# Moving TensorE's weight operands inside their SBUF buffers, in a chain of attention and two expert layers

## The chip, the core and the metric

The program runs on one NeuronCore of a Trainium2 chip. The metric is device time in microseconds (us) of one execution, from the first to the last instruction with what lies around them. Three timed executions of the kernel before stand beside one profiled execution, and the profile tells where the time of that one went.

## The reference

```python
def _attn_ref(q, k, v):                      # (4, 12, 448, 64) each
    scores = scale * np.matmul(q, k.transpose(0, 1, 3, 2)) - np.log(S)
    attn = 1.0 / (1.0 + np.exp(-scores))     # a sigmoid, no row sums
    return np.matmul(attn, v)

def _moe_ref(x, w1, w2, w3, w_out):          # x (1792, 768), weights (768, 768)
    h = np.maximum(np.maximum(x @ w1, x @ w2), x @ w3)
    return h @ w_out

def _moe2_ref(x, w_in, w_out):               # (768, 2048) and (2048, 768)
    h = x @ w_in
    g = h * (1.0 / (1.0 + np.exp(-1.702 * h)))
    return g @ w_out
```

Everything is float32. The output of the attention, put back to (1792, 768), runs through `_moe_ref` and then through `_moe2_ref`.

## The kernel before, in words

**Precision.** TensorE multiplies in the format float32r. Where that would lose too much, a matrix is kept as two float32r parts, `hi` and `lo`, and a product is three matmuls: hi by hi, hi by lo, lo by hi. Each matmul is preceded by its own load of 128 columns of weights (engine row PEld), and then 448 columns of the other operand are moved through. In this text the operand that is loaded is **the weight**, the other one is **the moving operand**; keys and v are weights of the attention, though they are data.

**Stages.** The 1792 tokens are four batches of 448. The attention runs over 24 pairs of heads. `score` (line 413 for two heads in two halves of the array, 415 for the last 64 keys of both) has keys as weights and queries as moving operand; both lie in one tile `qh` (and `ql`), the queries in columns 0 to 447, the keys from column S = 448 on. `weigh` has v as weights (`vs` with hi and lo side by side, lines 450 and 454; `v4` in plain float32, line 442, two records for each matmul) and the sigmoids `ah`, `al`, `a` as moving operand. Its result becomes the tiles `x0` to `x5` of a batch.

`unit1` and `unit2` are the first expert layers: `product` (lines 364 to 366) with weights `w1` and moving operands `x` or `h`, 18 matmuls for one bank of PSUM. `unit3` is the first half of the last layer: `product` again, with weights `w2` and moving operands `z`, which are read back from DRAM. `unit4` (lines 597 to 599) multiplies the gated result `g` by four-tile groups of `w2`; there are eight such groups, each used for the four batches in turn. The counts are 1296 matmuls on `x`, 432 on `h`, 1152 on `z` and 1152 on `g`, 216 with `vs` in full rows (line 450), 72 in half rows (454), 84 records of plain float32 (442), 432 half-row records of scores (413) and 72 full ones (415), and 10 to warm up (626).

**What sets the order.** All operations are first recorded in a class `Order`, with a guess of each one's time, and a list scheduler in `run` then issues them by due time on each engine; its guesses for a copy or a subtraction depend on the number of columns. A buffer ring that runs full makes the next tile's first writer wait.

**Places.** A tile is a stretch of every partition's bytes. Pools hand stretches out one after another, in multiples of 32 bytes. In the built program this gives the following places modulo 256 bytes (hi and lo, the 128-column slices of a weight, and the halves of the moving tiles are all whole multiples of 256 bytes apart, so one number tells a tile's place):

| weight by moving operand | weight | moving | weight minus moving |
|---|---|---|---|
| `w1` by `x`, `h` | 224 | 224 | 0 |
| `w2` by `z` of batch 0 | 192 | 192 | 0 |
| `w2` by `z` of batches 1 to 3 | 192 | 224 | -32 |
| `w2` by `g` | 192 | 192 | 0 |
| `vs` by `ah`, `al`; `v4` by `a` | 192 | 192 | 0 |
| keys by queries | 192 | 192 | 0 |

The `z` of batch 0 lie in another pool (`late`, on the left) than those of batches 1 to 3 (`acc`, on the right), which is why their places differ. The loop on which most of the time goes is, in `product`:

```python
pe.matmul(ps(), wh[:, c], xh, start=k == 0, stop=False)
pe.matmul(ps(), wh[:, c], lo(), start=False, stop=False)
pe.matmul(ps(), wl[:, c], xh, start=False, stop=k == KC - 1)
```

Of the kernel before, what the change touches and what calls it, by code (L numbers as in the profile page):

```python
# [7 lines left out]
F32 = mybir.dt.float32  # L8
F32R = mybir.dt.float32r
# [6 lines left out]
P = 128  # L16
B, H, S, D = 4, 12, 448, 64
DM = H * D
# [2 lines left out]
NF = DFF // P  # L21
NPAIR = H // 2
NP = B * NPAIR
QK = S + 3 * P + P
NW1 = 4 * KC
NW2 = 2 * NF

# [65 lines left out]
class Order:  # L93
# [6 lines left out]
    def ring(self, n, make, gate=None):  # L100
        r = Ring(n, make)
        r.gate = gate
        self.rings.append(r)
        return r
# [89 lines left out]
def moe_chain_kernel(tc, qk, vv, v4, wa, wb, out):  # L194
# [5 lines left out]
    def pool(name, bufs=1, **kw):  # L200
        return tc.alloc_tile_pool(name=name, bufs=bufs, **kw)

    def ring(p, name, shape, n, dtype=F32, gate=None):
        return O.ring(n, lambda: p[0].tile(shape, dtype, name=name, tag=name, bufs=n), gate)


    def dma(to, of, kb, reads, writes):
        return O.op({"SP": kb / 330.0}, lambda e: sp.dma_start(to().bitcast(F32), of().bitcast(F32)), reads, writes)

    def on(e, took, fn, reads, writes):  # L210
        return O.op({e: took}, lambda _: fn(), reads, writes)
# [11 lines left out]
    def rest(to, of, hi, n):  # L223
        return two(to, of, hi, ALU.subtract, n)
# [4 lines left out]
    xp = [pool("xp", side="right")]  # L229
# [4 lines left out]
    late, acc, pout = [None], [None], [None]  # L234

    def to_late(e):
        att[0].release()
        patt[0].release()
        late[0] = pool("late", side="left")
        pout[0] = pool("pout", space=PSUM)  # L240

    def to_acc(e):
# [6 lines left out]
    att_rings = [  # L249
        ring(att, *a)  # L250
        for a in (
            ("t", [P, QK], 2),
            ("qh", [P, QK], 2, F32R),
            ("ql", [P, QK], 2, F32R),
            ("a2", [P, 2, S], 5),
            ("a1", [P, S], 2),
            ("ah2", [P, 2, S], 4, F32R),
# [1 line left out]
            ("al2", [P, 2, S], 4, F32R),  # L259
            ("al1", [P, S], 2, F32R),  # L260
            ("vf", [P, 7, D], 1),
            ("vs", [P, 7, 2, D], 2, F32R),
            ("v4", [P, 11, D], 1),
            ("xf", [P, S], 2),
            ("fold", [D, S], 2),
# [1 line left out]
    ]  # L267
    ts, his, los, a2s, a1s, ah2s, ah1s, al2s, al1s, vfs, vss, v4s, xfs, folds = att_rings
    xs = [ring(xp, f"x{k}", [P, 2, S], 2, F32R) for k in range(KC)]
    w1s = ring(xp, "w1", [P, 2, DM], 4, F32R)  # L270
    hs = [ring(mid, f"h{k}", [P, 2, S], 1, F32R) for k in range(KC)]
    mxs = ring(mid, "mx", [P, S], 2)
    yst = ring(mid, "yst", [P, 2, S], 3, F32R)
# [1 line left out]
    def banks(p, name, n, shape=(P, 512)):  # L275
        return O.ring(n, lambda: p[0].tile(list(shape), F32, name=name, tag=name, bufs=n))

    scs, avs, mms = banks(patt, "sc", 2, (P, 2, 512)), banks(patt, "av", 2), banks(pmm, "mm", 2)
    pos = banks(pout, "po", 6)
    w2s = ring(late, "w2", [P, 2, DM], 7, F32R)  # L280
    z0s = [ring(late, f"z{k}", [P, 2, S], 1, F32R) for k in range(KC)]
    zs = [ring(acc, f"z{k}", [P, 2, S], B - 1, F32R) for k in range(KC)]
    gs = ring(late, "g", [P, 2, 2, S], 2, F32R)
    sgs = ring(late, "sg", [P, S], 2)
    gfs = ring(late, "gf", [P, S], 2)
    accs = ring(acc, "acc", [P, S], B * KC)
# [14 lines left out]
    def bank(r):  # L301
        return r.tile().part(lambda a: a[:, :S])

    def split(r):

        t = r.tile()
        return t.part(lambda a: a[:, 0]), t.part(lambda a: a[:, 1]), t

# [31 lines left out]
        rest(lo, y, hi, DM)  # L342

    def weights1(b, i):
        hi, lo, t = split(w1s)
        if b == 0:
            new_weights(wa[i], hi, lo)
            dma(kept[i], t, 768, [hi, lo], [kept[i]])
        else:
            dma(t, kept[i], 768, [kept[i]], [hi, lo])  # L350
        return hi, lo

    def weights2(i):
        hi, lo, _ = split(w2s)
        new_weights(wb[i], hi, lo)
        return hi, lo

# [15 lines left out]
    class Pair:  # L373
        def __init__(self, p):
            self.p, self.plain = p, p in PLAIN
            b, hp = divmod(p, NPAIR)
            t, self.h, self.l = ts.tile(), his.tile(), los.tile()
            cuts = [slice(0, S), slice(S, S + 2 * P), slice(S + 2 * P, QK)] if p == 0 else [slice(0, QK)]
            self.hi, self.lo = [], []
            for c in cuts:  # L380
                tp, hp_, lp = (z.part(lambda a, c=c: a[:, c]) for z in (t, self.h, self.l))
                n = c.stop - c.start
                O.op({"SP": n / 2 / 330.0}, lambda e, tp=tp, c=c: sp.dma_start(tp(), qk[p][:, c]), (), [tp])
                copy(hp_, tp, n)
                rest(lp, tp, hp_, n)
                self.hi.append(hp_)
                self.lo.append(lp)
            self.a, self.av = {}, None
            if self.plain:
                v = v4s.tile().part()  # L390
                O.op({"SP": 352 / 330.0}, lambda e: sp.dma_start(v(), v4[PLAIN.index(p)]), (), [v])
                self.v = [v]
            else:
                vf, vt = vfs.tile().part(), vss.tile()
                O.op({"SP": 224 / 330.0}, lambda e: sp.dma_start(vf(), vv[p]), (), [vf])
                vh, vl = (vt.part(lambda a, n=n: a[:, :, n, :]) for n in (0, 1))
                copy(vh, vf, 7 * D)
                rest(vl, vf, vh, 7 * D)
                self.v, self.vt = [vh, vl], vt

        def score(self, c):

            pair = c < 3
            ps = scs.tile().part((lambda a: a[:, :, :S]) if pair else (lambda a: a[:, 0, :S]))

            def f(_):
                o, h, l = ps(), self.h(), self.l()
                for n, (kx, qx) in enumerate(((h, h), (h, l), (l, h))):
                    how = dict(start=n == 0, stop=n == 2)
                    keys = slice(S + c * P, S + (c + 1) * P)  # L410
                    for e in range(2 if pair else 0):
                        r = slice(e * D, (e + 1) * D)
                        pe.matmul(o[:, e, :], kx[r, keys], qx[r, :S], **how)  # L413
                    if not pair:
                        pe.matmul(o, kx[:, keys], qx[:, :S], **how)  # L415

            used = (0, 1 + c // 2) if self.p == 0 else (0,)
            return f, 3 * MM, [x[i] for x in (self.hi, self.lo) for i in used], [ps]
# [146 lines left out]
    def unit3(u):  # L565
        grp, b = divmod(u, B)
        if b == 0:
            W[grp] = [weights2(4 * grp + j) for j in range(4)]
        if grp == 0:
            Z[b] = []  # L570
            for k in range(KC):
                hi, lo, t = split((zs if b else z0s)[k])
                dma(t, ykept[b][k], 448, [ykept[b][k]], [hi, lo])
                Z[b].append((hi, lo))
        t = gs.tile()
        gates[u] = []
        for j in range(2):
            ps = bank(mms)
            product(ps, W[grp][j], Z[b])
            sg, gf = sgs.tile().part(), gfs.tile().part()  # L580
            on("ACT", t_act(S), lambda sg=sg, ps=ps: act.activation(sg(), ps(), AF.Sigmoid, scale=1.702), [ps], [sg])  # L581
            two(gf, ps, sg, ALU.mult, S)
            hi, lo = (t.part(lambda a, j=j, n=n: a[:, j, n]) for n in (0, 1))
            copy(hi, gf, S)
            rest(lo, gf, hi, S)
            gates[u].append((hi, lo))
# [87 lines left out]
def _layout(i):  # L674
    import numpy as np

    q, k, v = (np.asarray(i[n]) for n in "qkv")
    qk = np.zeros((NP, 2, D, QK), q.dtype)
    qt, kt = (x.reshape(NP, 2, S, D).transpose(0, 1, 3, 2) for x in (q, k))
    qk[..., :S] = qt  # L680
    qk[..., S : S + 3 * P] = kt[..., : 3 * P]
    for e in range(2):
        qk[:, e, :, S + 3 * P + e * D :][..., :D] = kt[:, e, :, 3 * P :]
    v = v.reshape(NP, 2, S, D)
    vv = np.zeros((NP, P, 7, D), v.dtype)
    vv[:, :, :6] = v[:, :, : 3 * P].reshape(NP, 2, 3, P, D).transpose(0, 3, 2, 1, 4).reshape(NP, P, 6, D)
    vv[:, :, 6] = v[:, :, 3 * P :].reshape(NP, P, D)
    v4 = np.zeros((len(PLAIN), P, 11, D), v.dtype)
    for n, p in enumerate(PLAIN):
        a, b = v[p]  # L690
        for c in range(3):
            v4[n, :, 3 * c], v4[n, :, 3 * c + 2] = a[c * P : (c + 1) * P], b[c * P : (c + 1) * P]
        v4[n, :D, 9], v4[n, D:, 10] = a[3 * P :], b[3 * P :]
    w = [_tiles(_bits(i["moe_" + n])) for n in ("w1", "w2", "w3")]
    wa = np.stack(w, axis=1).reshape(3 * KC, P, DM)
    w_in = _tiles(_bits(i["moe2_w_in"])).reshape(NF // 2, 2, P, DM)
    w_out = _bits(i["moe2_w_out"]).reshape(NF // 2, 2, P, DM)
    return {
        "qk": qk.reshape(NP, P, QK),
        "vv": vv,  # L700
        "v4": v4,
        "wa": np.concatenate([wa, _tiles(_bits(i["moe_w_out"]))]),
        "wb": np.concatenate([w_in, w_out], axis=1).reshape(NW2, P, DM),
    }
# [22 lines left out]
```

## Time and profile before

| what | value |
|---|---|
| three timed executions | 1000.32, 1002.26, 1002.57 us; median 1002.26 |
| profiled execution, its own time | 1004.32 us |
| its span, first to last instruction | 1002.5 us |
| granted TensorE clock, mean | 1.000 |
| PE busy / PEld busy | 987.9 / 872.3 us |
| DVE / ACT busy | 621.9 / 347.1 us |

PE is TensorE's matmuls, PEld its weight loads (they overlap PE), DVE is VectorE, ACT is ScalarE, SP issues the transfers. An "x" before a number is a count. A matmul's record is longer than the time until the next matmul starts, since matmuls are pipelined: where they run back to back, the time per matmul (called **the pace** here) is the distance from start to start, and it is read from a stretch by dividing its length by the number of matmuls that start in it.

### The profile page before, as it was taken

The page shows a single profiled execution, that of the slowest core. Times are in us where ns is not written, and L with a number is a line of the kernel's source. Part 1 is how long each engine was busy: PE and PEld are TensorE (multiplying, and loading weights), DVE is VectorE, ACT ScalarE, POOL GpSimd, SP SyncE. Part 2 cuts the span into 40 slices and gives each one's busy share as a digit, 9 for nine tenths or more (in the row PEclk, how much of TensorE's full clock was granted, in tenths as well). Part 3 has the DMA queues.
Part 4 walks back from the last instruction along what each step waited for, and adds up shares of the span by engine and source line. Part 5 has one row for each costly group of instructions (what it writes and reads, how often), then busy time and mean ns, then how long its engine had stood idle before and what let it go on. Part 6 is the DMA issues. An engine that isn't in the chain of part 4 may idle for free.

```text
span 1002.5 us, 12196 instructions
## 1 busy us (share of the span) xinstructions
PE 987.9 (99%) x4918; PEld 872.3 (87%) x4918; DVE 621.9 (62%) x945; ACT 347.1 (35%) x514; POOL 1.1 (0%) x6
## 2 busy tenths in 40 slices
PE   8899999999999999999999999999999999999998
PEld 5568887888888889999998999999999999999997
DVE  7989998997576747511112355767747576754344
ACT  6666665953454532110012331221222122221110
POOL 0000000000000000000000000000000000000000
PEclk9999999999999999999999999999999999999999
DMA  7866686996555659896668111110201111000023
GB/s 253 298 206 237 247 306 250 352 379 218 184 201 178 217 182 395 307 350 213 214 206 319 48 63 64 63 63 1 95 32 63 63 64 63 1 1 1 1 99 123
DMA packets 39656, 165.95 MB, mean 166 GB/s; under 512 B 4400, under 2 KB 10288, under 8 KB 39600
## 3 DMA queue, kind: packets, MB, share of 16 engines
q1 hardware_dynamic: 39600, 165.17, 45.9%
q8 instruction: 39, 0.64, 0.3%
q14 instruction: 17, 0.14, 0.0%
HBM read 129.76 MB, written 35.39 MB: 165 GB/s over the span
## 4 chain that ended last, share of the span: by engine, by line
PE 91%; DMA 4%; DVE 3%; issue 1%; ACT 1%; SPq 0%; DVEq 0%
PE mm L364 19%; PE mm L366 19%; PE mm L365 19%; PE po L598 8%; PE po L599 8%; PE po L597 8%; PE sc L413 4%; PE av L450 4%; PE av L442 3%; DMA raw<-in_wa 2%; PE sc L415 1%; PE av L454 1%; DMA v<-in_v 1%; DVE y L337 1%; DVE al L221 0%
## 5 line engine op out<-in xcount | busy, mean ns | idle before, releaser
L364 PE MATMUL mm<-x,w 128*128 128x448 f32 x432 | 162.1, 375 | 0.0
L365 PE MATMUL mm<-x,w 128*128 128x448 f32 x432 | 158.6, 367 | 0.0
L366 PE MATMUL mm<-x,w 128*128 128x448 f32 x432 | 158.6, 367 | 0.0
L221 DVE TENSOR_TENSOR acc<-po,acc 128x448 f32<-128x448 f32 (+1 forms) x169 | 103.9, 620 | 62.7 <-PE po L599 61.5
L364 PE MATMUL mm<-z,w 128*128 128x448 f32 x384 | 141.5, 368 | 1.1 <-DMA z<-yk 1.1
L366 PE MATMUL mm<-z,w 128*128 128x448 f32 x384 | 141.1, 368 | 0.0
L365 PE MATMUL mm<-z,w 128*128 128x448 f32 x384 | 141.1, 367 | 0.0
L598 PE MATMUL po<-g,w 128*128 128x448 f32 x384 | 140.3, 365 | 0.0
L599 PE MATMUL po<-g,w 128*128 128x448 f32 x384 | 140.2, 365 | 0.0
L597 PE MATMUL po<-g,w 128*128 128x448 f32 x384 | 140.2, 365 | 0.0
L581 ACT ACTIVATE sg<-mm 128x448 f32<-128x448 f32 x64 | 34.8, 544 | 252.1 <-PE mm L366 252.0
L423 ACT ACTIVATE a<-sc,bias 128x896 f32<-128x896 f32 (+1 forms) x96 | 85.0, 913 | 55.6 <-PE sc L413 43.6
L221 DVE TENSOR_TENSOR gf<-mm,sg 128x448 f32<-128x448 f32 x64 | 39.9, 623 | 88.6 <-ACT sg L581 87.4
L364 PEld LDWEIGHTS mm<-x,w 128*128 128x128 f32 x432 | 81.1, 188 | 14.8 <-issue 7.3
L366 PEld LDWEIGHTS mm<-x,w 128*128 128x128 f32 x432 | 81.1, 188 | 7.7
L365 PEld LDWEIGHTS mm<-x,w 128*128 128x128 f32 x432 | 81.2, 188 | 7.6 <-issue 0.6
L221 DVE TENSOR_TENSOR mx<-mm,mx 128x448 f32<-128x448 f32 x48 | 29.9, 624 | 88.3 <-PE mm L366 88.1
L364 PEld LDWEIGHTS mm<-z,w 128*128 128x128 f32 x384 | 72.2, 188 | 8.2 <-issue 1.4
L366 PEld LDWEIGHTS mm<-z,w 128*128 128x128 f32 x384 | 72.2, 188 | 6.8
L365 PEld LDWEIGHTS mm<-z,w 128*128 128x128 f32 x384 | 72.2, 188 | 6.6
L597 PEld LDWEIGHTS po<-g,w 128*128 128x128 f32 x384 | 72.1, 188 | 5.8
L598 PEld LDWEIGHTS po<-g,w 128*128 128x128 f32 x384 | 72.1, 188 | 5.7
(77 smaller groups left out, 1399.8 us busy)
## 6 DMA issues: line engine op xcount, KB each, us to landing
w<-kept SPq DMA_DIRECT2D x72, 768.0 KB, 4.7
raw<-in_wb SPq DMA_DIRECT2D x32, 768.0 KB, 5.2
raw<-in_wa SPq DMA_DIRECT2D x24, 768.0 KB, 4.8
kept<-w SPq DMA_DIRECT2D x24, 768.0 KB, 4.1
t<-in_qk SPq DMA_DIRECT2D x23, 480.0 KB, 4.0
yk<-yst SPq DMA_DIRECT2D x24, 448.0 KB, 5.6
z<-yk SPq DMA_DIRECT2D x24, 448.0 KB, 8.3
out_t<-acc SPq DMA_DIRECT2D x23, 224.0 KB, 1.9
```

What stands on the lines that cost most here:

```text
L221: return on("DVE", t_two(n), lambda: dve.tensor_tensor(to(), a(), b(), op=op), [a, b], [to])
L364: pe.matmul(ps(), wh[:, c], xh, start=k == 0, stop=False)
L365: pe.matmul(ps(), wh[:, c], lo(), start=False, stop=False)
L366: pe.matmul(ps(), wl[:, c], xh, start=False, stop=k == KC - 1)
L413: pe.matmul(o[:, e, :], kx[r, keys], qx[r, :S], **how)
L423: on("ACT", t_act(n) + 0.07, lambda: act.activation(a(), ps(), AF.Sigmoid, bias=bias, scale=scale), [ps], [a])
L442: pe.matmul(o, w, x[:, e, :] if c < 3 else x, start=c + e == 0, stop=c == 3)
L450: pe.matmul(av[e](), w, x()[:, e, :], start=c + n == 0, stop=False)
L581: on("ACT", t_act(S), lambda sg=sg, ps=ps: act.activation(sg(), ps(), AF.Sigmoid, scale=1.702), [ps], [sg])
L597: pe.matmul(ps(), wh[:, c], gh, start=j == 0, stop=False)
L598: pe.matmul(ps(), wh[:, c], gl, start=False, stop=False)
L599: pe.matmul(ps(), wl[:, c], gh, start=False, stop=j == 1)
```

## The change

Weights get a fixed distance from their moving operand. `w1`, `w2` and `vs` tiles are 64 elements (256 bytes) longer, and their contents begin OFF = 48 elements, that is 192 bytes, into them. `t`, `qh` and `ql` rows grow to a multiple of 256 bytes; 16 empty columns (64 bytes) stand between queries and keys, so the transfers of queries and keys and the two operations that split them have 976 columns in place of 960. A tile `space` of 32 bytes at the head of the pool `late` moves all that follows it by 32 bytes, so that the `z` of batch 0 lie at 224 like the others. `g` tiles are 256 bytes longer, and the contents begin at an offset that depends on the group of weights: G_OFF, in elements.

```diff
-QK = S + 3 * P + P
+KEYS = S + 16
+QK = KEYS + 3 * P + P
+
+OFF = 48
+G_OFF = (0, 8, 16, 24, 32, 40, 4, 60)
...
         late[0] = pool("late", side="left")
+        late[0].tile([P, 8], F32, name="space")
...
-            ("t", [P, QK], 2),
-            ("qh", [P, QK], 2, F32R),
-            ("ql", [P, QK], 2, F32R),
+            ("t", [P, QK + 48], 2),
+            ("qh", [P, QK + 48], 2, F32R),
+            ("ql", [P, QK + 48], 2, F32R),
...
-            ("vs", [P, 7, 2, D], 2, F32R),
+            ("vs", [P, 14 * D + 64], 2, F32R),
...
-    w1s = ring(xp, "w1", [P, 2, DM], 4, F32R)
+    w1s = ring(xp, "w1", [P, 2 * DM + 64], 4, F32R)
...
-    w2s = ring(late, "w2", [P, 2, DM], 7, F32R)
+    w2s = ring(late, "w2", [P, 2 * DM + 64], 7, F32R)
...
-    gs = ring(late, "g", [P, 2, 2, S], 2, F32R)
+    gs = ring(late, "g", [P, 4 * S + 64], 2, F32R)
...
+    def weight_tile(r):
+        t = r.tile()
+        of = lambda n: t.part(lambda a: a[:, OFF + n * DM :][:, :DM])
+        return of(0), of(1), Part(t, lambda a: a[:, OFF:][:, : 2 * DM].rearrange("p (t n) -> p t n", t=2))
...
-                    keys = slice(S + c * P, S + (c + 1) * P)
+                    keys = slice(KEYS + c * P, KEYS + (c + 1) * P)
...
-            hi, lo = (t.part(lambda a, j=j, n=n: a[:, j, n]) for n in (0, 1))
+            hi, lo = (t.part(lambda a, j=2 * j + n: a[:, G_OFF[grp] + j * S :][:, :S]) for n in (0, 1))
```

In the built program the places are then, modulo 256 bytes:

| weight by moving operand | weight | moving | weight minus moving |
|---|---|---|---|
| `w1` by `x`, `h`; `w2` by `z` of all batches | 160 | 224 | -64 |
| `vs` by `ah`, `al` | 128 | 192 | -64 |
| keys by queries | 0 | 192 | 64 |
| `v4` by `a` | 192 | 192 | 0 |
| `w2` by `g`, groups 0 to 5 | 160 | 224, 0, 32, 64, 96, 128 | -64, -96, -128, 96, 64, 32 |
| `w2` by `g`, groups 6 and 7 | 160 | 240, 208 | -80, -48 |

The number of matmuls, of other operations and of transfers is unchanged, and a weight tile is still one transfer of 6144 bytes for each partition. Since the splits of queries and keys are guessed longer, the scheduler puts three products of the expert layers at another place among the attention's matmuls, and some splits on DVE and ACT one or two rows away. The first such place on PE is in the first expert layer of batch 0, beside the `weigh` of a pair with `vs`. Before (a number behind a name tells one tile from another):

```order
L364 MATMUL mm<-x_222,w_393 128x448
L365 MATMUL mm<-x_222,w_393 128x448
L366 MATMUL mm<-x_222,w_393 128x448
L450 MATMUL av<-ah_666,vs 128x448 x2
L450 MATMUL av<-al_678,vs 128x448 x2
L450 MATMUL av<-ah_714,vs 128x448 x2
L450 MATMUL av<-al_722,vs 128x448 x2
L450 MATMUL av<-ah_732,vs 128x448 x2
L450 MATMUL av<-al_738,vs 128x448 x2
L364 MATMUL mm<-x_353,w_393 128x448
```

And the same place now:

```order
L374 MATMUL mm<-x_222,w_393 128x448
L375 MATMUL mm<-x_222,w_393 128x448
L376 MATMUL mm<-x_222,w_393 128x448
L374 MATMUL mm<-x_367,w_393 128x448
L375 MATMUL mm<-x_367,w_393 128x448
L376 MATMUL mm<-x_367,w_393 128x448
L461 MATMUL av<-ah_666,vs 128x448 x2
L461 MATMUL av<-al_678,vs 128x448 x2
L461 MATMUL av<-ah_714,vs 128x448 x2
L461 MATMUL av<-al_722,vs 128x448 x2
```

One product of three matmuls stands ahead of the twelve matmuls of `weigh` that it stood behind. The other two moves are of the same kind, one product past some 25 rows.

## Rows read from the trace of the kernel before

**Rows 1.** The page: span, and busy time of each engine.

```profile
span 1002.5 us, 12196 instructions
PE 987.9 (99%) x4918; PEld 872.3 (87%) x4918; DVE 621.9 (62%) x945; ACT 347.1 (35%) x514; POOL 1.1 (0%) x6
```

**Rows 2.** The page: the chain that ended last, by engine.

```profile
PE 91%; DMA 4%; DVE 3%; issue 1%; ACT 1%; SPq 0%; DVEq 0%
```

**Rows 3.** Busy time in stretches of the span: length, then engines, clock, DMA.

```profile
150.00:200.00 50.00, 48.37 (x255) 41.70 (x255) 46.30 (x65) 37.25 (x54) 0.00 (x0) 1.00 0.80 299
400.00:536.00 136.00, 134.93 (x655) 122.40 (x654) 33.88 (x53) 18.45 (x33) 0.00 (x0) 1.00 0.72 254
600.00:800.00 200.00, 200.00 (x982) 184.14 (x981) 133.06 (x213) 44.05 (x70) 0.00 (x0) 1.00 0.16 56
```

**Rows 4.** Busy time of PE alone in one stretch of `x` and `h` by `w1`.

```profile
368.23:526.50 158.27, 158.27 (x767) 1.00 0.78 281
```

**Rows 5.** Timeline of PE: start, length, line; another stretch of `x` by `w1`.

```profile
147.18 0.36 PE L366 MATMUL mm<-x,w 128*128 128x448 f32 x1
...
157.52 0.36 PE L366 MATMUL mm<-x,w 128*128 128x448 f32 x1
```

**Rows 6.** Timeline of PE: `z` of batch 0 by `w2`, then `g` by `w2`.

```profile
580.61 0.36 PE L364 MATMUL mm<-z,w 128*128 128x448 f32 x1
...
587.30 0.36 PE L597 MATMUL po<-g,w 128*128 128x448 f32 x1
...
593.38 0.37 PE L364 MATMUL mm<-z,w 128*128 128x448 f32 x1
```

**Rows 7.** Timeline of PE: `z` of batch 1 by the same `w2` tiles.

```profile
595.22 0.36 PE L364 MATMUL mm<-z,w 128*128 128x448 f32 x1
...
602.03 0.36 PE L597 MATMUL po<-g,w 128*128 128x448 f32 x1
```

**Rows 8.** Timeline of all engines: a matmul and the next weight load start together.

```profile
411.21 0.37 PE L364 MATMUL mm<-x,w 128*128 128x448 f32 x1
411.21 0.19 PEld L365 LDWEIGHTS mm<-x,w 128*128 128x128 f32 x1
```

**Rows 9.** The chain in order of time: plain float32 matmuls, two records each.

```profile
28.56 3.27 PE av L442 x8
...
59.78 4.78 PE av L442 x12
```

**Rows 10.** Groups by line and shape: count, busy us, mean ns of one.

```profile
L365 PE MATMUL mm<-x,w 128*128 128x448 f32 x432 | 158.6, 367 | 0.0
...
L365 PE MATMUL mm<-z,w 128*128 128x448 f32 x384 | 141.1, 367 | 0.0
...
L599 PE MATMUL po<-g,w 128*128 128x448 f32 x384 | 140.2, 365 | 0.0
...
L450 PE MATMUL av<-al,vs 128*128 128x448 f32 x108 | 30.7, 366 | 0.0
...
L413 PE MATMUL sc<-ql,qh 64*128 64x448 f32 x144 | 26.6, 362 | 0.0
...
L221 DVE TENSOR_TENSOR ql<-t,qh 128x960 fp32r<-128x960 f32 x23 | 26.5, 1152 | 0.0
...
L454 PE MATMUL av<-al,vs 64*128 64x448 f32 x36 | 6.7, 360 | 0.0
...
L218 DVE CAST qh<-t 128x960 fp32r<-128x960 f32 x13 | 8.5, 658 | 1.4 <-PE sc L415 1.4
```

**Rows 11.** Transfers of queries and keys: count, KB each, us to landing.

```profile
t<-in_qk SPq DMA_DIRECT2D x23, 480.0 KB, 4.0
```

**Rows 12.** PE in the first 200 us: line 366 alone, then line 450 alone.

```profile
0.00:200.00 200.00, 52.73 (x144) 1.00 0.75 268
...
0.00:200.00 200.00, 19.93 (x86) 1.00 0.75 268
```

More of the change, by code (lines that the diff above doesn't have):

```diff
@@ L344, in weights1 @@
     def weights1(b, i):
-        hi, lo, t = split(w1s)
+        hi, lo, t = weight_tile(w1s)
         if b == 0:
@@ L353, in weights2 @@
     def weights2(i):
-        hi, lo, _ = split(w2s)
+        hi, lo, _ = weight_tile(w2s)
         new_weights(wb[i], hi, lo)
@@ L377, in __init__ @@
             t, self.h, self.l = ts.tile(), his.tile(), los.tile()
-            cuts = [slice(0, S), slice(S, S + 2 * P), slice(S + 2 * P, QK)] if p == 0 else [slice(0, QK)]
+            cuts = [slice(0, KEYS), slice(KEYS, KEYS + 2 * P), slice(KEYS + 2 * P, QK)] if p == 0 else [slice(0, QK)]
             self.hi, self.lo = [], []
@@ L395, in __init__ @@
                 O.op({"SP": 224 / 330.0}, lambda e: sp.dma_start(vf(), vv[p]), (), [vf])
-                vh, vl = (vt.part(lambda a, n=n: a[:, :, n, :]) for n in (0, 1))
+                v2 = lambda a: a[:, OFF:][:, : 14 * D].rearrange("p (c t d) -> p c t d", t=2, d=D)
+                vh, vl = (vt.part(lambda a, n=n: v2(a)[:, :, n, :]) for n in (0, 1))
                 copy(vh, vf, 7 * D)
                 rest(vl, vf, vh, 7 * D)
-                self.v, self.vt = [vh, vl], vt
+                self.v, self.vt = [vh, vl], lambda: v2(vt())
         def score(self, c):
@@ L680, in _layout @@
     qk[..., :S] = qt
-    qk[..., S : S + 3 * P] = kt[..., : 3 * P]
+    qk[..., KEYS : KEYS + 3 * P] = kt[..., : 3 * P]
     for e in range(2):
-        qk[:, e, :, S + 3 * P + e * D :][..., :D] = kt[:, e, :, 3 * P :]
+        qk[:, e, :, KEYS + 3 * P + e * D :][..., :D] = kt[:, e, :, 3 * P :]
     v = v.reshape(NP, 2, S, D)
```

## The prediction, made before the changed kernel ran

> **What bounds the kernel now.** I read the page's busy times first: PE works 987.9 of 1002.5 us, no other engine more than 622 [rows 1]. The chain of waits says the same from the other side: 91% of what ended last is PE, 4% transfers, 3% DVE [rows 2]. Then the table by stretches: from 600 us on PE is never idle, DVE works 133 of 200 us and the transfers run at 0.16 of their engines; from 400 to 536 us they run at 0.72, and PE still has only 1 us idle in 136 [rows 3]. Only early is anything else close: from 150 to 200 us DVE works 46.3 of 50 us beside PE's 48.4. So for some 800 of the 1002 us the time is the number of matmuls times their pace, and the granted clock is 1.00, the level of 2.4 GHz, throughout.
>
> The pace is not one number. 448 columns at one a cycle would take 448/2.4 = 187 ns (an estimate, from the shape and the granted clock). What the trace shows is this. `x` and `h` by `w1`, at distance 0: 158.27 us for 766 matmuls (the 767th was under way), 206.6 ns [rows 4]. The same line, the same places, earlier: 10.34 us for 51, 202.7 ns [rows 5]. `z` of batch 0 by `w2`, distance 0: 6.69 us for 33, 202.7 ns; then `g`, distance 0: 6.08 us for 30, 202.7 ns [rows 6]. `z` of batch 1 by the very same weight tiles, distance -32 bytes: 6.81 us for 33, 206.4 ns [rows 7]. So every matmul loses 16 to 20 ns over the estimate, and how much depends a little on places: rows 6 and 7 differ in nothing else that I can find. The loss belongs to full speed: plain float32 records, at distance 0 too, take (4.78 - 3.27)/4 = 0.377 us each [rows 9], twice 187 ns and 3 ns more. And each matmul starts in the same 10 ns as the next weight load [rows 8], so the two read SBUF side by side, each matmul anew.
>
> **The change, part by part.**
>
> *Weights 64 bytes behind the moving operand (`w1`, `w2` by `z`, `vs`).* No row shows this distance, so it has to be bounded. Below: 187 ns, the columns alone. Above: the step from distance 0 to -32 cost up to 206.4 - 202.7 = 3.7 ns [rows 6, 7]; another step like it gives 210 ns. Between them I go by the nearest rows that are neither of the two paces. A matmul's record is 162 ns longer than its pace where the run is unbroken (`g`: 365 against 202.7 [rows 6, 10]); by this the half-row records, 362 for scores and 360 for `v`, stand at 198 to 200 ns [rows 10]. I take 199 ns. The bet in it: the two distances whose pace is known are neighbours, 32 of 256 bytes apart, and stand at 203 to 207, so more of the room between floor and ceiling lies below them than above.
>
> The sum: `x` and `h`, 1728 matmuls at 367 - 162 = 205 ns [rows 10], to 199: -6 x 1728 = -10.4 us. `z`, 1152 matmuls; three batches at 206.4 and one at 202.7 make 205.5: -6.5 x 1152 = -7.5 us. `vs`, 216 full-row matmuls at 366 - 162 = 204: -5 x 216 = -1.1 us. Together -19.0 us. At the floor the three would give -31.1, -21.3 and -3.7, -56 us; at the ceiling of 210 ns +8.6, +5.2 and +1.3, +15 us.
>
> *`g`, by group.* Eight groups of 144 matmuls stand at eight distances from -128 to 96 bytes. One of them is that of the main part, the others are unseen. Some should gain and some lose; I take 0 against 202.7 ns. Bounds: -15.7 x 1152 = -18.1 us at the floor, +7.3 x 1152 = +8.4 us at the ceiling.
>
> *Keys 64 bytes from the queries.* 432 half-row matmuls go in pairs, 216 slots, and 72 full ones: 288 slots at about 200 ns [rows 10]. I take 0; bounds -13 x 288 = -3.7 and +10 x 288 = +2.9 us.
>
> *Queries and keys 16 columns longer.* DVE's subtraction takes 1152 ns for 960 columns, its copy 658 [rows 10]: 19 and 11 ns more, on 24 pairs at most 0.7 us of DVE, all in the attention, where DVE is busiest [rows 3]. The transfer grows from 480 to 488 KB; at 4.0 us to landing [rows 11] that is under 0.1 us, hidden by the second `t` buffer. I take +0.5 us in all. If the cover is gone, it is 0.7 + 24 x 0.1 = +3 us.
>
> *Order.* Three products change places with `weigh` matmuls on PE. The same matmuls run, and no transfer moves with them; what comes later is one bank of scores' results by 0.6 us, less than the rings of `a` tiles hold. I take 0, bounds -1 and +1 us.
>
> *What the faster PE meets.* In the first 200 us, with DVE at 46 of 50 us [rows 3], a faster PE would find DVE in its way. Of the matmuls above, 3 x 144 products' and 86 of `vs` run there [rows 12]: 518 x 6 ns = 3.1 us, and since PE is busier still than DVE, I take back half, 1.5 us (bounds 0 and 3).
>
> Sum: -19.0 + 0.5 + 1.5 = -17.0 us. From the profiled execution's own 1004.32 us that is 987.3; the median of the three runs is 2.06 us under that execution, so I say **985 us**. In the later stages nothing else comes near: at 199 ns the stretch from 600 to 800 us would be 6 us shorter and DVE's 133 us still fit.
>
> **The rivals.**
>
> *One step further in the wrong direction.* From distance 0 to -32 the pace rose from 202.7 to 206.4; if what causes this grows with the distance, -64 lies at 206 to 210 ns. At 210 the terms above give +15 us, and the three groups of `g` near it (-48, -64, -80) +7 x 432 = +3 us, the other five half as much a matmul, +2.6; with +0.5 for the columns, +21 us: 1023. At 207, +2 x 1728 + 1.5 x 1152 + 3 x 216 = +5.8 us, with half the `g` at 207 +2.5: 1011. This decides for slower wherever the pace in rows 4's stretch does not fall below 205 ns. For it: the only step in the trace goes this way. Against it: that step is one of eight around 256 bytes, and distance 0 itself shows 206.6 as well as 202.7. I say 1016 for it, chance 0.22.
>
> *The moving operand's own place decides, not the distance.* Then moving the weights does nothing, and what matters is that `z` of batch 0 goes from 192 to 224 and `g` from 192 to eight places. At 206.4 where a place is 32 bytes off a multiple of 64: `z` of batch 0, 288 x 3.7 = +1.1 us; `g` groups 0, 2 and 4, 432 x 3.7 = +1.6 us; groups 6 and 7 unknown, 0 to +1.1 us; columns +0.5: +3.2 to +4.3 us, 1006. For it: rows 6 and 7 differ in the place of `z` and have the same weights. Against it: rows 5 has 202.7 with the moving operand at 224. Chance 0.15. The Trainium skill speaks for this one (TensorE: Matmul & The Clock Gate, "Step-by-step: what each phase is for"): TensorE has two independent read ports of SBUF, and loading the next weights takes no bandwidth from the running matmul. By that rule the distance could do nothing and the result would be the 1006 just worked out; rows 6 and 7 neither refute nor need it, and no row shows the two reads apart.
>
> *Neither decides; a run of matmuls keeps the pace it fell into.* Rows 4 and 5 are the same places at two paces. If the change only deals these anew, 1728 matmuls could go from 205 to 202.7 (-4 us) or to 206.6 (+2.8 us), and the others likewise by a little: 998 to 1006. That is the change not doing what it says. Chance 0.18.
>
> **How the numbers follow.** Forecast, a pace clearly under 202 ns in the main part: 0.45. The rivals: 0.22, 0.15, 0.18. A measurement of this kernel tells 0.2%, 2 us, from no change. Faster by more: 0.45 + 0.07 from the third rival = 0.52. Slower: 0.22 + 0.11 + 0.05 = 0.38. Within: the rest, 0.10. The floor of all terms together, -56 - 18 - 4 = -78 us, is 924 us, but no row comes near 187 ns, so the low end is a pace of some 187 to 190 for half of the work, about -50 us: 950 us. The high end cuts the first rival between its 1011 and its 1023: 1016. The forecast's own range is 950 to 998.
>
> **What would show it.** Right: in the stretch of rows 4 the length divided by the count is near 199 ns, the records of the `x`, `z` and `vs` rows in the view by line are near 361 ns, and `g` shows one pace per group. The first rival: records of 369 to 372 there. The second: `x` unchanged at 367, `z` of batch 0 at 369, and the groups of `g` sorted by their own place, not by the distance. The third: two paces in one line at one place, as now. PE idle much above the 14.6 us it has (span less busy [rows 1]), most of it before 200 us behind DVE, would say that the pace fell and another engine took it back.

## The result, and the profile after

| kernel | median, us | lowest to highest | runs |
|---|---|---|---|
| before | 1002.41 | 1000.32 to 1003.20 | 4 |
| changed | 987.73 | 987.43 to 988.07 | 4 |

The ratio is 0.9857, with a 95% interval of 0.9840 to 0.9874: **faster by 14.7 us**. The profiled execution of the changed kernel took 987.43 us, its span 985.6, at a granted clock of 1.000.

The page of the changed kernel: span, busy times, the chain by engine, and the transfers of queries and keys.

```profile
span 985.6 us, 12195 instructions
...
PE 972.6 (99%) x4918; PEld 871.3 (88%) x4918; DVE 621.8 (63%) x945; ACT 347.5 (35%) x514; POOL 1.1 (0%) x6
...
PE 95%; DVE 2%; DMA 1%; issue 0%; SPq 0%; ACT 0%; DVEq 0%
...
t<-in_qk SPq DMA_DIRECT2D x23, 488.0 KB, 4.3
```

The other engines and the number of matmuls stand as before [rows 1]; PE alone lost 15.3 us of busy time, and its idle time went from 14.6 to 13.0 us. So the gain of 16.9 us between the two spans is on PE, and the chain is PE's even more than before (95%, before 91% [rows 2]). The transfers of queries and keys land in 4.3 us in place of 4.0 [rows 11]. No wait of PE is put down to them; those of DVE and ACT come to 9.6 us, before 9.1.

The stretches of [rows 3] in the changed kernel (length, then busy time and count of PE, PEld, DVE, ACT, POOL, granted clock, transfers):

```profile
150.00:200.00 50.00, 50.00 (x269) 44.38 (x268) 48.60 (x69) 38.73 (x55) 0.00 (x0) 1.00 0.86 323
400.00:536.00 136.00, 134.75 (x675) 125.98 (x674) 33.21 (x53) 19.77 (x36) 0.00 (x0) 1.00 0.76 271
600.00:800.00 200.00, 200.00 (x993) 186.03 (x992) 133.79 (x215) 46.49 (x73) 0.00 (x0) 1.00 0.14 48
```

From 150 to 200 us PE now is busy throughout and issues 269 matmuls where it issued 255, and DVE, at 48.6 of 50 us, keeps up. From 400 to 536 us it is 675 for 655. From 600 to 800 us only 993 for 982, because there half of the matmuls are `g`.

PE alone in a stretch of `x` and `h` by `w1`, to be held against [rows 4]:

```profile
368.23:500.00 131.77, 131.77 (x660) 1.00 0.82 300
```

659 matmuls start in it (the 660th was under way): 131.77/659 = 200.0 ns, before 206.6.

The timeline of PE in the changed kernel (start, length, line): first `x` by `w1`, then `z` of batch 0, `g` of the batch before it, and `z` of batch 1, which is followed by the next group's `g`.

```profile
145.73 0.36 PE L374 MATMUL mm<-x,w 128*128 128x448 f32 x1
...
155.93 0.36 PE L374 MATMUL mm<-x,w 128*128 128x448 f32 x1
...
568.36 0.36 PE L374 MATMUL mm<-z,w 128*128 128x448 f32 x1
...
574.96 0.36 PE L608 MATMUL po<-g,w 128*128 128x448 f32 x1
...
580.96 0.36 PE L374 MATMUL mm<-z,w 128*128 128x448 f32 x1
...
582.76 0.36 PE L374 MATMUL mm<-z,w 128*128 128x448 f32 x1
...
589.36 0.37 PE L608 MATMUL po<-g,w 128*128 128x448 f32 x1
```

The first two rows are 10.20 us and 51 matmuls apart, 200.0 ns where [rows 5] gave 202.7. `z` of batch 0 takes 6.60 us for 33, and `z` of batch 1 6.60 us for 33: 200.0 ns both, where [rows 6, 7] had 202.7 and 206.4. `g` of group 0 takes 6.00 us for 30, 200.0 ns. At distance -64 all these stretches run at this one pace, in patterns that repeat every three matmuls: 197, 202, 201 ns in `x`, 198, 201, 201 ns in `z` and `g`.

The groups by line and shape (count, busy us, mean ns of one), to be held against [rows 10]:

```profile
L375 PE MATMUL mm<-x,w 128*128 128x448 f32 x432 | 156.6, 363 | 0.0
...
L375 PE MATMUL mm<-z,w 128*128 128x448 f32 x384 | 139.4, 363 | 0.0
...
L610 PE MATMUL po<-g,w 128*128 128x448 f32 x384 | 140.0, 365 | 0.0
...
L461 PE MATMUL av<-al,vs 128*128 128x448 f32 x108 | 30.5, 363 | 0.0
...
L424 PE MATMUL sc<-ql,qh 64*128 64x448 f32 x144 | 26.7, 364 | 0.0
```

The records of `x` and `z` fell by 4 ns, those of `vs` by 3, `g` kept its mean, and the half-row scores rose from 362 to 364.

What hides in the mean of `g` is seen group by group. PE's `g` matmuls alone, 30 that follow each other in one batch of each group; the groups' distances are -64, -96, -128, 96, 64, 32, -80 and -48:

```profile
560.56:566.56 6.00, 6.00 (x30) 1.00 0.01 3
603.95:610.10 6.15, 6.15 (x30) 1.00 0.00 0
662.28:668.39 6.11, 6.11 (x30) 1.00 0.01 3
720.39:726.41 6.02, 6.02 (x30) 1.00 0.00 0
778.26:784.33 6.07, 6.07 (x30) 1.00 0.00 0
836.34:842.47 6.13, 6.13 (x30) 1.00 0.00 0
894.54:900.63 6.09, 6.09 (x30) 1.00 0.01 3
952.61:958.70 6.09, 6.09 (x30) 1.00 0.31 114
```

Over all four batches of a group these are 200.0, 205.0, 203.8, 200.9, 202.6, 204.4, 203.0 and 202.9 ns, a mean of 202.8. Before, all were at 202.7 [rows 6].

Summed from start to start over the whole trace, waits included, by what the matmuls move:

| matmuls | before, us | after, us | difference | forecast |
|---|---|---|---|---|
| `x` and `h` | 366.2 | 355.5 | -10.7 | -10.4 |
| `z` | 238.0 | 232.2 | -5.8 | -7.5 |
| `ah`, `al` by `vs` | 55.7 | 55.1 | -0.6 | -1.1 |
| `g` | 233.3 | 233.4 | +0.1 | 0 |
| queries by keys | 69.3 | 69.4 | +0.1 | 0 |

### The profile page after: what moved, and what is told of

Its sections match the earlier page's. It is cut to its first block, busy times and chain, and to the rows that moved or that the text cites. A ratio compares the mean times of both kernels' runs of the same rounds, so it can differ in the third digit from the quotient of the medians.

```text
span 985.6 us, 12195 instructions
## 1 busy us (share of the span) xinstructions
PE 972.6 (99%) x4918; PEld 871.3 (88%) x4918; DVE 621.8 (63%) x945; ACT 347.5 (35%) x514; POOL 1.1 (0%) x6
## 4 chain that ended last, share of the span: by engine, by line
PE 95%; DVE 2%; DMA 1%; issue 0%; SPq 0%; ACT 0%; DVEq 0%
PE mm L374 20%; PE mm L376 19%; PE mm L375 19%; PE po L608 8%; PE po L609 8%; PE po L610 8%; PE sc L424 4%; PE av L461 4%; PE av L453 3%; PE sc L426 1%; DMA raw<-in_wa 1%; PE av L465 1%; DMA v<-in_v 1%; DVE al L225 0%; DVE y L347 0%
## 5 line engine op out<-in xcount | busy, mean ns | idle before, releaser
L374 PE MATMUL mm<-x,w 128*128 128x448 f32 x432 | 159.5, 369 | 0.0
L376 PE MATMUL mm<-x,w 128*128 128x448 f32 x432 | 156.9, 363 | 0.0
L375 PE MATMUL mm<-x,w 128*128 128x448 f32 x432 | 156.6, 363 | 0.0
L374 PE MATMUL mm<-z,w 128*128 128x448 f32 x384 | 138.9, 362 | 1.2 <-DVE gf L225 1.2
L375 PE MATMUL mm<-z,w 128*128 128x448 f32 x384 | 139.4, 363 | 0.0
L376 PE MATMUL mm<-z,w 128*128 128x448 f32 x384 | 138.9, 362 | 0.0
L374 PEld LDWEIGHTS mm<-z,w 128*128 128x128 f32 x384 | 72.0, 187 | 7.0 <-issue 1.6
L610 PEld LDWEIGHTS po<-g,w 128*128 128x128 f32 x384 | 72.1, 188 | 5.8
L608 PEld LDWEIGHTS po<-g,w 128*128 128x128 f32 x384 | 72.0, 188 | 5.8
L609 PEld LDWEIGHTS po<-g,w 128*128 128x128 f32 x384 | 72.1, 188 | 5.7
L375 PEld LDWEIGHTS mm<-z,w 128*128 128x128 f32 x384 | 72.1, 188 | 5.1
```

What stands on the lines that cost most here:

```text
L608: pe.matmul(ps(), wh[:, c], gh, start=j == 0, stop=False)
L609: pe.matmul(ps(), wh[:, c], gl, start=False, stop=False)
L610: pe.matmul(ps(), wl[:, c], gh, start=False, stop=j == 1)
```

## The experiments

Three theories stood against each other: the **distance** between weight and moving operand sets the pace; the **moving operand's own place** sets it; or a **stretch keeps a pace it fell into**, whatever the places. Where a table gives a pace, it is the mean interval between full-row matmuls that follow each other without a wait. Kernels with one run have no interval, and their times are given to place them, not to rank them within 1 us.

### All of `g` at -64

```diff
-G_OFF = (0, 8, 16, 24, 32, 40, 4, 60)
+G_OFF = (0,) * 8
```

> The changed kernel with all eight offsets of g at 0, so that g stands 64 bytes ahead of its weights in every group, as x, h and z do. Theory (distance between weight and moving operand sets the pace): g goes from a mean of 202.8 ns to the 200.0 ns that group 0 showed, 1008 matmuls in seven groups by 3.2 ns = -3.2 us, 984.5 us against 987.7. Rival (the moving operand's own place decides): the same, since all g then lie at 224 like group 0. Rival (a run keeps the pace it fell into): groups fall to 200 or 203 to 207 without order, and the time stays within 1 us of 987.7.

Measured: 984.24 us (983.79 to 984.83, 5 runs) beside 1002.96 for the kernel before, ratio 0.9814 [0.9801, 0.9828]. All eight groups run at 200.0 ns. PE in the stretch from 600 to 800 us:

```profile
600.00:800.00 200.00, 200.00 (x1001) 1.00 0.14 48
```

1000 matmuls start in 200 us, where the changed kernel had 992. The span is 982.1, 3.5 us less, and 1152 x (202.8 - 200.0) = 3.2 us. So the offset by group costs 3.5 us of the 18.7 that this version gains on the kernel before, and this one-line version **beats both kernels**.

### The same distances, made by moving the weights

The moving `g` stays at 224, and the weights of the second half of the layer move instead.

```diff
-G_OFF = (0, 8, 16, 24, 32, 40, 4, 60)
+G_OFF = (0,) * 8
+W_OFF = (48, 40, 32, 24, 16, 8, 44, 52)
...
-    def weight_tile(r):
+    def weight_tile(r, OFF=OFF):
...
-        hi, lo, _ = weight_tile(w2s)
+        hi, lo, _ = weight_tile(w2s, OFF if i % 4 < 2 else W_OFF[i // 4])
```

> All g at 224, and instead the weights of w_out at eight places by group, so that the distances are those of the changed kernel, group by group, with the other operand moved. Distance theory: the pace of g by group is that of the changed kernel within 0.5 ns: 200.0, 205.0, 203.8, 200.9, 202.6, 204.4, 203.0, 202.9. Rival (the moving operand's own place decides): all eight groups at 200.0. Rival (a run keeps its pace): no agreement group by group.

Measured: 988.33 us, one run. Four stretches of `g` in that trace, 30 matmuls each, at -64, -96, 96 and 64:

```profile
561.35:567.35 6.00, 6.00 (x30) 1.00 0.01 3
604.75:610.90 6.15, 6.15 (x30) 1.00 0.00 0
721.11:727.10 5.99, 5.99 (x30) 1.00 0.00 0
778.79:784.87 6.08, 6.08 (x30) 1.00 0.00 0
```

| distance | -64 | -96 | -128 | 96 | 64 | 32 | -80 | -48 |
|---|---|---|---|---|---|---|---|---|
| moving operand moved (the change) | 200.0 | 205.0 | 203.8 | 200.9 | 202.6 | 204.4 | 203.0 | 202.9 |
| weight moved | 200.0 | 205.2 | 203.8 | 199.9 | 202.4 | 204.0 | 203.5 | 204.3 |

At -64 the two kernels have the same places. Of the seven distances made at different places six agree within 1.0 ns; -48 differs by 1.5. If the moving operand's own place decided, the second row would be one number. That theory falls. So does the one that the weight's own place decides: in the first row the weights lie at 160 in every group. The distance decides nearly all, but 96 and -48 already say not quite all. Whether the places themselves count a little was not tested.

### Without the 32 bytes at the head of the pool

As the first experiment, but `z` of batches 1 to 3 then stand 32 bytes further from their weights (-96), while `z` of batch 0 and `g` keep -64.

```diff
-        late[0].tile([P, 8], F32, name="space")
```

> As the first run, but without the 32-byte tile at the head of the late pool: w2 weights at 128, g and z of batch 0 at 192 (distance -64), z of batches 1 to 3 at 224 as they were (distance -96). Distance theory: z of batch 0 and g at 200 ns, z of batches 1 to 3 at 205 ns, the pace that g showed at -96; 864 matmuls by 4.8 ns = +4.1 us against the first run, 988.6 us. Rival (the moving operand's own place decides): z of batches 1 to 3 stays at 200.3 ns, since its place does not change, and the time is that of the first run.

Measured: 989.13 us (988.24 to 991.78, 4 runs), ratio 0.9866 [0.9852, 0.9881]. PE's matmuls with `w2` tiles in that trace, first `z` of batch 3, then the `g` behind it (one matmul of each count was under way at the start):

```profile
554.75:561.52 6.77, 6.77 (x34) 1.00 0.00 0
561.52:567.53 6.01, 6.01 (x31) 1.00 0.01 3
```

33 matmuls of `z` start in 6.77 us, 205.1 ns, and 30 of `g` in 6.01, 200.3 ns. The mean of `z` of batches 1 to 3 is 205.0 ns, that of batch 0 stays at 200. The price, 4.9 us between the medians, is 864 matmuls of `z` at 205.0 - 200.0 ns = 4.3 us, and 1152 of `g` at 200.4 - 200.0 = 0.5 us. 32 bytes in front of a pool are worth more than all that the groups of `g` cost.

### Sixteen more distances

`g` at eight other distances, in two kernels.

```diff
-G_OFF = (0, 8, 16, 24, 32, 40, 4, 60)
+G_OFF = (1, 2, 62, 20, 28, 36, 44, 52)
```

> The changed kernel with other offsets of g by group, for distances -68, -72, -56, 112, 80, 48, 16, -16 bytes. Distance theory with a smooth dependence: -68, -72 and -56 within 2 ns of the 200.0 of -64, 80 between the 200.9 of 96 and the 202.6 of 64, and the others between 201 and 207; the whole within 2 us of the changed kernel. A theory of whole 16-byte or 64-byte pieces instead has steps: -68, -72 and -56, which begin inside a piece of 16 bytes, clearly worse (over 204) than -64 and -80.

```diff
-G_OFF = (0, 8, 16, 24, 32, 40, 4, 60)
+G_OFF = (12, 54, 50, 58, 42, 26, 22, 46)
```

> The changed kernel with other offsets of g by group, for distances -112, -24, -8, -40, 24, 88, 104, 8 bytes, to look for a pace under 200.0 ns. So far sixteen distances give 200.0 to 207.9 and three of them exactly 200.0 (-64, -16, and the second half of each unit at 96). If 200.0 is a floor for this shape, none of the eight goes below it. If the pace varies freely with the distance, one or two of eight new ones should be below 199.

Measured: 989.88 and 989.99 us, one run each. Four stretches of `g` in the first, at -68, -72, -56 and -16:

```profile
562.28:568.52 6.24, 6.24 (x30) 1.00 0.01 3
606.25:612.38 6.13, 6.13 (x30) 1.00 0.00 0
664.47:670.57 6.10, 6.10 (x30) 1.00 0.01 3
941.00:947.00 6.00, 6.00 (x30) 1.00 0.31 115
```

With the change's own eight, and 0 and -32 from before, the pace by distance in bytes is, in ns:

| -128 | -112 | -96 | -80 | -72 | -68 | -64 | -56 | -48 |
|---|---|---|---|---|---|---|---|---|
| 203.8 | 206.5 | 205.0 | 203.0 | 204.4 | 207.9 | **200.0** | 203.4 | 202.9 |

| -40 | -32 | -24 | -16 | -8 | 0 | 8 | 16 |
|---|---|---|---|---|---|---|---|
| 203.0 | 206.4 | 204.5 | **200.0** | 205.7 | 202.7 or 206.7 | 203.4 | 202.6 |

| 24 | 32 | 48 | 64 | 80 | 88 | 96 | 104 | 112 |
|---|---|---|---|---|---|---|---|---|
| 206.5 | 204.4 | 203.9 | 202.6 | 204.2 | 205.5 | 200.9 | 206.5 | 205.9 |

Nothing smooth runs through this: 4 bytes off -64 cost 8 ns, the dearest step of all. Steps of 16 bytes do not explain it either: of the distances in whole 16 bytes 96 is good and 32 is not, and of the others -56 and 8 are as good as -80. And nothing is clearly below 200.0; the lowest is the 199.9 of 96 with the weight moved.

### Distance 0 for all but the keys, with everything else of the change

As the first experiment, with the longer buffers and the 32 bytes, but the weights at the head of their tiles. The keys stay at +64.

```diff
-OFF = 48
+OFF = 0
```

> The first run (all g at one place) with OFF = 0: everything else of the change stays, the longer buffers, the 32-byte tile, the space before the keys, but weights and moving operands of all expert layers stand at the same place, 224, distance 0. Distance theory: the paces of distance 0 come back: x and h 205.4 ns as before, z and g somewhere between the 202.7 and the 206.7 that distance 0 showed, vs 203.6: +9.0, +3 to +7.5, +3 to +7.5 and +0.8 us on 984.2 us, 1000 to 1009 us. A theory that the buffers' lengths or the 32-byte tile brought the gain: stays near 984 us.

Measured: 997.06 us (994.72 to 1007.80, 10 runs), ratio 0.9957 [0.9927, 0.9987]. This is under what was expected, and the trace says why. PE in the stretch of `x` and `h`, then `z` followed by `g`:

```profile
368.23:500.00 131.77, 131.77 (x652) 1.00 0.81 297
...
560.70:567.39 6.69, 6.69 (x35) 1.00 0.00 0
567.39:573.47 6.08, 6.08 (x32) 1.00 0.01 3
```

The first is 131.77/651 = 202.4 ns, and the others 6.69/33 and 6.08/30, both 202.7 ns: nearly the whole of `z`, `g` and this stretch fell into the better of the two paces that distance 0 has, where before this very stretch was at 206.6 [rows 4]. Elsewhere the worse one is still there: over the whole trace `x` and `h` stand at 203.7 and 203.5. So the third theory is right **at distance 0**: the same places have two patterns, steady at 206.7, or five intervals of 202, 203, 202, 199 and 207 that come to 202.7, and a stretch keeps the one that it is in. But against the first experiment the three kinds of matmul are 1728 x 3.4 + 1152 x 2.7 + 1152 x 2.7 = 12.1 us slower, and the medians, taken on two chips, are 12.8 apart. The place of the weights alone brings these; longer buffers and the 32 bytes do not.

### What is the floor of 200 ns made of?

448 columns at 2.4 GHz are 186.7 ns, so 13.3 are left. First half the load: groups 3 to 6 of `g` load 64 columns of weights in place of 128.

```diff
+FULL = (0, 1, 2, 7)
...
-            ps, c = bank(pos), slice(o * P, (o + 1) * P)
+            ps, c = bank(pos), slice(o * P, (o + 1) * P if grp in FULL else o * P + 64)
```

> The first run, but in groups 3 to 6 of the last layer each matmul on g loads 64 columns of weights in place of 128 and gives 64 rows (the other 64 rows of the result are left out for these groups, and so is their addition). The moving operand is unchanged. If the 13 ns above the estimate of 187 ns come from the load's reads beside the moving operand's, half the load leaves about half of them: 192 to 195 ns in these groups, 200.0 in the others. If the moving operand's own reads cost them, or the hand-over from one matmul to the next does, the pace stays at 200 ns.

Measured: 984.75 us, one run. Two stretches of 30 matmuls of `g`, with 128 and with 64 columns of weights, then the loads by line and shape:

```profile
661.28:667.28 6.00, 6.00 (x30) 1.00 0.01 3
718.96:725.00 6.04, 6.04 (x30) 1.00 0.00 0
...
L612 PEld LDWEIGHTS po<-g,w 128*128 128x128 f32 x192 | 36.0, 188 | 2.6
...
L612 PEld LDWEIGHTS po<-g,w 128*64 128x64 f32 x192 | 25.7, 134 | 13.2
```

A load's record falls from 188 to 134 ns, and the pace does not fall at all: over whole groups it is 201.6 ns with half a load, 200.0 with a whole one. So, at this distance, what a matmul loses is not in proportion to what the load reads, and the pace of 200 is not set by the load's own length.

Then fewer moving columns: groups 1 to 6 move 416, 416, 384, 384, 320 and 320.

```diff
+WIDE = (S, 416, 416, 384, 384, 320, 320, S)
...
+                    gh, gl, to = gh[:, :wide], gl[:, :wide], ps()[:, :wide]
```

> The first run, but the matmuls on g move only 416 columns in groups 1 and 2, 384 in groups 3 and 4, 320 in groups 5 and 6 (the columns beyond are left out of those groups' sums). At the estimate of one column a cycle of 2.4 GHz these are 173.3, 160.0 and 133.3 ns. If the loss is a fixed cost of each matmul, 13.3 ns as at 448 columns: 186.7, 173.3, 146.7. If it grows with the moved columns (7.1%): 185.7, 171.4, 142.9. If the next load, whose record is 188 ns, sets the time: no faster than about 190 ns in any of them. Widths between these rules say that the load takes over below a certain width.

Measured: 957.73 us, one run. `g` stretches with 448, 416, 384 and 320 columns:

```profile
560.48:566.48 6.00, 6.00 (x30) 1.00 0.01 3
603.27:608.92 5.65, 5.65 (x30) 1.00 0.00 0
714.80:720.00 5.20, 5.20 (x30) 1.00 0.00 0
821.37:825.77 4.40, 4.40 (x30) 1.00 0.00 0
```

| columns | pace, ns | columns / 2.4 GHz | what is left |
|---|---|---|---|
| 448 | 200.0 | 186.7 | 13.3 |
| 416 | 188.5 | 173.3 | 15.2 |
| 384 | 173.3 | 160.0 | 13.3 |
| 320 | 146.5 | 133.3 | 13.2 |

At the good distance a matmul of 448, 384 or 320 columns costs its columns and a fixed 13.3 ns, 32 of the 2.4 GHz cycles, down to a pace below the 188 ns of the load's record. 416 columns cost 1.9 ns more than that, and why was not found. The Trainium skill (TensorE: Matmul & The Clock Gate, "Back-to-back issue gap") has N/2.4 + 2.5 ns for an isolated matmul, without the load at small N, and says that this over-counts at large N; the trace, with a load before every matmul, shows 13.3 and not 2.5, more and not less. What the 32 cycles are was not found.

### Does the hi or the lo weight's distance count?

The distance of hi weights and that of lo weights were set apart: hi at -16, the second of the two good ones, lo at -16, -68, 104 and 24 for two groups each.

```diff
+HI = 60
+LO = (60, 60, 47, 47, 26, 26, 6, 6)
...
+    def out_tile(r, lo):
+        t = r.tile()
+        return t.part(lambda a: a[:, HI : HI + DM]), t.part(lambda a: a[:, 64 + DM + lo :][:, :DM])
```

> The first run, with the hi weights of w_out at distance -16 (which held 200.0 ns in every interval) and the lo weights at -16, -68, 104 and 24 bytes in groups 0-1, 2-3, 4-5, 6-7 (which alone gave 200.0, 207.9, 206.5, 206.5). Of three matmuls two use hi weights, the third lo. If the load that runs beside a matmul is what matters, the second of the three (beside it the lo weights are loaded) leaves 200.0 first; if a matmul's own weights matter, the third. By distance alone, one third of the intervals at the bad value: 200.0, 202.6, 202.2, 202.2 ns on the mean.

Measured: 987.54 us, one run. A stretch of `g` of group 0, 30 matmuls with hi and lo at -16:

```profile
561.20:567.30 6.10, 6.10 (x30) 1.00 0.01 3
```

**This told nothing of its question, and something else**: the base itself, hi and lo both at -16, ran at 203.0 and 202.9 ns in its two groups, not at the 200.0 that -16 had given with the moving operand at another place. The others stood at 202.4 (-68), 202.9 (104) and 202.3 (24), though alone these distances gave 207.9, 206.5 and 206.5. So a distance can have more than one pace, at -16 as at 0 and at -48, and what picks the pattern (the absolute place, the place of the lo part, or what ran before) stays open. -64, with 448 columns and whole loads, gave 200.0 to 200.5 for `x`, `h`, `z` and `g` in every kernel that has it, and 200.9 to 201.0 for the few matmuls with `vs`.

### Keys at -64 too

The keys are the one weight that the change puts at +64. Here they stand at -64, for which 32 more columns lie between queries and keys; the rows of `t`, `qh` and `ql` keep their length. The second run sets the kernel beside the first experiment's on one chip.

```diff
-KEYS = S + 16
+KEYS = S + 48
```

> The first run with 48 empty columns between queries and keys in place of 16, so that the keys stand at distance -64 from the queries, like the other weights, in place of +64. A pair of half-row score matmuls takes 202.0 ns now. If the distance acts there as in full rows: from the 202.6 of +64 to the 200.0 of -64, 250 slots by 2 ns = -0.5 us, and the 32 longer columns of the splits cost up to +1 us: 983.5 to 985.5 us, a difference that can't be told from none. If two half-row tiles at once behave in another way, a pair takes 204 ns or more, or 198 or less.

> The first run's kernel once more, beside the next one: 984.2 us as there, 0.981 of the time before.

> The kernel with 48 empty columns before the keys once more, beside the one above on the same chip. Score pairs at 201.1 ns against 202.0 would give -0.2 us, the longer splits up to +1 us: within 1 us of the kernel above. If the 987 us measured before were its own and not its chip's, it is 2 to 3 us slower, and the wait for it is in the first 400 us, where scores, splits and DVE are.

Measured: 987.07 us (986.06 to 990.03, 4 runs, beside 1002.43); then 986.82 (986.43 to 988.06, 5 runs) beside 984.49 (982.79 to 984.82, 4 runs) for the first experiment's kernel. Pairs of score matmuls go from 202.0 to some 201.4 ns, 0.1 us in all, and the kernel is 2.3 us slower. Two stretches early on, keys at +64 first:

```profile
25.00:50.00 25.00, 22.13 (x99) 13.32 (x95) 23.60 (x33) 17.12 (x23) 0.00 (x0) 1.00 0.81 300
50.00:100.00 50.00, 48.35 (x243) 37.17 (x244) 45.35 (x65) 31.81 (x42) 0.00 (x0) 1.00 0.66 223
```

And with keys at -64:

```profile
25.00:50.00 25.00, 22.33 (x96) 13.38 (x93) 22.69 (x32) 17.81 (x22) 0.00 (x0) 0.93 0.77 275
50.00:100.00 50.00, 47.51 (x237) 35.75 (x236) 42.84 (x61) 32.38 (x43) 0.00 (x0) 1.00 0.61 215
```

PE has issued 9 matmuls less between 25 and 100 us, nearly 2 us, but it was idle only 0.6 us more. Two of PE's waits in the first 100 us differ by more than 0.1 us; with keys at +64 they are (us in total, times, longest):

```profile
PE av L453 <- DVE xf L487: 2.8, 2, 1.7
...
PE av L453 <- DMA v<-in_v: 1.2, 1, 1.2
```

With keys at -64 the second one is gone, and the first is:

```profile
PE av L453 <- DVE xf L487: 4.4, 2, 2.6
```

The splits' guessed times grew by 32 columns, the scheduler put two more instructions on ACT (516 for 514, DVE 943 for 945), and PE's waits for this tile of DVE are 1.6 us longer, of which the missing wait for `v` gives 1.2 back. In this execution the rest goes with the clock: a mean granted clock of 0.93 over 25 us is 3.5 us at the 1.2 GHz level, in a stretch in which PE had waited, and PE's busy time over the whole span is 970.7 us for 969.3. The clock is not the cause by itself, since another execution with keys at -64 kept 1.000 and took the same 986.43 us. So what costs the 2.3 us stays open; order, length of the splits and clock were not taken apart.

## Why the prediction was right

**Direction, time and mechanism held.** 985 us were forecast and 987.7 came, and the cause was the one named: one pace in the main part, clearly under 202 ns, and set, nearly, by the distance. That the spans differ by 16.9 us where the sum said 17.0 is luck: the paces gave 15.3 us, not 19.0, nothing of the 2.0 us was given back, and a wait of 1.6 us, of which the sum knew nothing, went away.

- *The pace at -64.* 199 ns forecast, 200.0 to 200.3 measured (200.9 for `vs`). The way there was luckier than it looks. I read 198 to 200 ns from half-row records, taking 162 ns off; but pairs of score matmuls really took 202.9 ns before, and when the change brought them to 201.8 the record that I had read rose from 362 to 364. Those rows did not show a pace of 200 at all. What held was the other half of the argument, that two neighbouring distances out of the 256 bytes, both at 203 to 207, leave more room below than above. Of the 26 distances in the tables 2 lie at 200.0, 1 at 200.9 and 23 over 202; their mean is 204. No distance is clearly better than -64, and most would have given a third of its gain or less. That the one taken is among the best is luck: the prediction had no reason for -64.
- *`x` and `h`* -10.4 forecast, -10.7 measured, but the pace gave only 9.0 of it: 200.3 in place of 199, from 205.5 in place of 205, is 5.2 x 1728. The rest is the wait that went away. *`z`* -7.5 forecast, -5.8 measured: 200.3 in place of 199 and 205.3 before in place of 205.5. *`vs`* half of the -1.1.
- *`g`* 0 forecast, +0.1 measured, by cancelling of groups from 200.0 to 205.0, as it was put.
- *Keys, columns, order.* +0.1 us for the queries by keys; of the +0.5 us for longer splits nothing is seen. The last experiment shows that this could have gone otherwise: the kernel with 32 columns more and another order was 2.3 us slower, for a reason that stays open.
- *Giving back 1.5 us to DVE* did not happen: PE's idle time fell by 1.6 us, and from 150 to 200 us PE is at 50.0 of 50 with DVE at 48.6. DVE was closer to PE than anyone, and still not in its way. PE's idle time there before, which the prediction read beside DVE's 46.3 us, was one wait, and for ACT:

```profile
PE sc L415 <- ACT a L423: 1.6, 1, 1.6
```

The changed kernel has no such wait. Whether its order or the faster PE took it away is not shown.

- *From 600 to 800 us* the prediction's 6 us are too many by its own terms: only the `z`, some 480 of 980 matmuls there, were to gain 6.5 ns each, 3 us. It came to 11 matmuls, 2.2 us.
- *From one execution to the median.* Span against span the change gave 16.9 us, the sum said 17.0. The median of before was 1.9 us under its profiled execution and that of the changed kernel 0.3 over its own, and this is most of the 2.7 us by which 987.7 missed 985. The four runs of before spread over 2.9 us and those after over 0.6; the ten with weights at distance 0 spread over 13.1. This fits two paces at distance 0 that each execution mixes anew; that is argued, not shown.

**The rivals.** *One step further in the wrong direction* had the only visible step on its side, and fell: from 0 to -32 to -64 it is 202.7, 206.4, 200.0. Its mistake would have been a straight line through two points of something that jumps. *The moving operand's own place* fell to the mirrored kernel and to the 32 bytes of the pool. The prediction weighed a rule with it (the Trainium skill, TensorE: Matmul & The Clock Gate, "Step-by-step: what each phase is for"): loading the next weights takes no SBUF read bandwidth from the running matmul. By that rule the place of the weights could do nothing, and here it does: with `x` where it was, 64 bytes of shift in its weights took it from 205.5 to 200.3 ns. Whether bandwidth is what is lost is not shown: half the load did not shorten the pace. *Neither decides* is true of distance 0 and worth some 3 us there, as the kernel at distance 0 showed (`x` and `h`, at their old places, at 203.7 ns for 205.5); it was counted as a rival of the distance, and is a property of some distances.

## What to carry to other kernels

Where PE is never idle and each matmul has its own weight load, divide a stretch by its count: if the pace of such matmuls (float32r, 320 to 448 columns here) is over columns/2.4 GHz + 13 ns, the places of weight and moving operand modulo 256 bytes are worth a sweep. Sweep it with one kernel that gives groups of matmuls different distances, read the pace of each group, then put the best one everywhere; a rule guessed from two or three distances will mislead. Watch what else the shift does: a few bytes at the head of a pool move every tile behind it, and padding that lengthens an operation's shape changes what the scheduler does with it.

## What was not expected of the hardware

- The pace depends on the distance in jumps: 207.9 ns at -68 bytes, 200.0 at -64, 203.4 at -56.
- No distance goes clearly below 200.0 ns for 448 columns (lowest: 199.9); 13.3 ns a matmul remain with 384 and 320 columns too, 15.2 with 416, and with half the load 14.9.
- Some distances have several patterns: 202.7 or 206.7 at 0, 200.0 or 203.0 at -16, 202.9 or 204.3 at -48, 200.9 or 199.9 at 96. So the distance is not the whole state, and what else belongs to it is open.
- A weight load's record of 188 ns is no lower bound for the pace: matmuls of 384 and 320 columns, each with such a load, followed each other every 173.3 and 146.5 ns.
